# A list scheduler that plans with spare time for transfers and for the engines beside TensorE

## Chip, core and metric

The kernel runs on one core of a Trainium2 chip. The metric is device time in microseconds (us), the median of three runs. TensorE (PE) does the matmuls, VectorE (DVE), ScalarE (ACT) and GpSimd (POOL) do the element-wise work, and SyncE (SP) does no arithmetic here: its queue issues the transfers (DMA), one after the other.

## What is computed

```python
# attention with a feature map, 4 batches x 8 heads x 576 positions x 64
phi = lambda x: [exp(p), exp(-p)], p = x @ w_phi - max|x @ w_phi|
x = (phi(q) @ (phi(k).T @ v)) / (phi(q) @ sum(phi(k)))     # -> 2304 x 512
# mixture of 4 experts, weighted by p = domain_probs / sum
out += p[:, e:e+1] * (relu(x @ w1[e]) @ w2[e])             # 512 -> 1024 -> 512
# gated block
y = ((out @ v1) * (out @ v2)) @ w3 @ w_out                 # -> 2304 x 512
```

## The kernel before

The program is written as a list of operations, each with an engine, an estimated duration and the tiles it reads and writes. `Prog.run` plays that list through a small event model (`simulate`) three times and emits the instructions in the order in which the last pass started them. Every engine then works through its own instructions strictly in that order. So the numbers in the model never run on the chip; they only decide what stands behind what.

In the first pass the model takes ready operations by their place in the text. After that, `deadlines` works out for every operation of DVE, ACT, POOL and SP when it is due, backwards from the PE operations that need it, and the next pass takes ready operations by that due time, PE keeping the order of the pass before. A transfer takes its issue time on SP (400 ns), then lands after `BEFORE` + bytes/`RATE` + `AFTER` ns, where the byte counts are partly fitted numbers and not sizes. A tile is taken when its first writer starts and given back after its last reader, so the order decides also when buffers come free.

The stages: attention in the first 200 us, mixed with the first visits of the experts. A visit is one quarter of an expert (visits 0 to 50 with fold steps among them) for one or two pairs of 768 tokens: PE computes `upa`, `upb`, `upc` (seven products instead of eight, so sums are formed by DVE and ACT: tiles `s1`, `s2`, `s5`, lines L865 and L872), ACT and DVE make `h` from them (L897, L899), PE multiplies by the second weights into `dn` (L911), and DVE adds that to `acc` (L932). Weights come by `raw_a`, `raw_b`, `raw_g` (L431, three buffers for all of them) and are split in two parts by ACT (cast, L421) and POOL (L423, with sums L451) into `w_a`, `w_b`, `w_g`. Fold visits multiply w3 by w_out (`psw`, L1012), because the gated block has no function between them. The last visits (51 to 58) are the gated block.

Three kinds of side work are laid among this. The weights of the gated block arrive as 64-bit numbers; 40 half tiles are brought to 32 bits: a load `near` (L463), one ACT step (L466), five DVE steps (L469, L472, L476, L479, L482) and a write `near_v`, `near_w` or `near_wo` back to memory (L485). They are worked on in buffers named `near0` (24 halves), `near1` and `near2` (8 each). The sums of an expert pair, once complete, are transposed in 32x32 blocks by DVE (L940) and written by four strided transfers each (`turned`, L944, 24 for a pair), then loaded back as `xr` (L948). From `xr` ACT and DVE split the tokens into `x..` tiles (L421, L423, L755).

Of the kernel before, what the change touches and what calls it, by code (L numbers as in the profile page):

```python
# [108 lines left out]
class Op:  # L109
    def __init__(self, n, eng, ns, fn, prio, size, port, mode):  # L110
        self.n, self.eng, self.ns, self.fn, self.prio, self.port, self.size = n, eng, ns, fn, prio, port, size
        self.mode = mode
        self.lag = Prog.TAIL.get(eng, 0.0)
        self.values, self.deps, self.next = [], set(), []


class Prog:
# [10 lines left out]


    SYNC = 45.0  # L130
    TAIL = {"PE": 275.0, "DVE": 185.0, "ACT": 200.0, "POOL": 185.0}
    BEFORE, AFTER, RATE, MARGIN = 850.0, 550.0, 330.0, 400.0
    COLD = 4500.0
# [30 lines left out]
    def simulate(self, key, same=0):  # L164

        for o in self.ops:
            o.count = len(o.deps)
            for v in o.values:
                v.left, v.live = 0, False
        for o in self.ops:  # L170
            for v in o.values:
                v.left += 1
        free, turn = {k: [None] * n for k, n in self.bufs.items()}, dict.fromkeys(self.lines, 0)
        self.heirs, slots = {}, dict.fromkeys(self.bufs, -1)
        engines = list(dict.fromkeys(o.eng for o in self.ops))
        ready, busy, port = {e: [] for e in engines}, dict.fromkeys(engines, 0.0), dict.fromkeys(self.OTHER, 0.0)
        mode = [None]
        events, done, served = [(0.0, 0, o.n, o) for o in self.ops if not o.count], [], [0.0]
        heapq.heapify(events)

        def fits(o):
            need, lines = {}, {}
            for v in o.values:
                if not v.live and v.args[2] is not None:
                    k, n = need.get(v.key, 0), lines.get(v.line, 0)
                    if len(free[v.key]) <= k or v.order != turn[v.line] + n:
                        return False
                    need[v.key], lines[v.line] = k + 1, n + 1
            return True

        def take(o, now):
            for v in o.values:
                if not v.live:
                    v.live = True
                    turn[v.line] += 1
                    v.slot = slots[v.key] = slots[v.key] + 1
                    if v.args[2] is not None:
                        self.heirs[free[v.key].pop(0)] = v
            o.start, o.end = now, now + o.ns
            if o.eng == "PE" and now < self.COLD:  # L200
                o.end += min(o.ns, (self.COLD - now) / 2)
            if o.eng == "PE" and o.mode != mode[0]:
                o.end += self.SWITCH
                mode[0] = o.mode
            busy[o.eng] = o.end
            if o.port:
                port[o.eng] = now + o.port if o.port > 1 else o.end - self.EARLY[o.eng]
            if o.eng == "SP":
                served[0] = max(o.end + self.BEFORE, served[0]) + o.size / self.RATE
                o.lag = served[0] + self.AFTER - o.end  # L210
            done.append(o)
            heapq.heappush(events, (o.end, 2, o.n, o))
            heapq.heappush(events, (o.end + o.lag, 1, o.n, o))

        def choose(e, now):
            held, late, got = [], None, None
            while ready[e] and got is None:
                item = heapq.heappop(ready[e])
                if not fits(item[2]):
                    held.append(item)  # L220
                elif item[2].port and port[self.OTHER[e]] > now:
                    if late is None:
                        late = item
                    else:
                        held.append(item)
                else:
                    got = item
            if got is None and late is not None:
                got, late = late, None
            if late is not None:  # L230
                held.append(late)
            if same and e == "PE" and got is not None and got[2].mode != mode[0]:
                near = [x for x in ready[e] if x[0] <= got[0] + same and x[2].mode == mode[0] and fits(x[2])]
                if near:
                    held.append(got)
                    got = min(near)
                    ready[e].remove(got)
                    heapq.heapify(ready[e])
            for item in held:
                heapq.heappush(ready[e], item)  # L240
            return got and got[2]

        while events:
            now = events[0][0]
            while events and events[0][0] <= now:
                _, kind, _, o = heapq.heappop(events)
                if kind == 0:
                    heapq.heappush(ready[o.eng], (key(o), o.n, o))
                elif kind == 1:
                    for v in o.values:  # L250
                        v.left -= 1
                        if not v.left:
                            free[v.key].append(v)
                    for x in o.next:
                        x.count -= 1
                        if not x.count:
                            heapq.heappush(events, (now + self.SYNC, 0, x.n, x))
            again = True
            while again:
                again = False  # L260
                for e in engines:
                    if busy[e] <= now and ready[e]:
                        o = choose(e, now)
                        if o is not None:
                            take(o, max(now, port[self.OTHER[e]]) if o.port else now)
                            again = True
        assert len(done) == len(self.ops), (len(done), len(self.ops))
        return done
# [15 lines left out]
    def deadlines(self, reuses):  # L284
        due = {}
        for o in sorted(self.ops, key=lambda o: (-o.start, -o.n)):
            t = o.start if o.eng == "PE" else float("inf")
            for x in (*o.next, *reuses[o]):
                if x in due:
                    t = min(t, due[x] - o.ns - o.lag - self.SYNC - (self.MARGIN if o.eng == "SP" else 0.0))  # L290
            due[o] = t
# [47 lines left out]
def fused_kernel(ctx, tc, qT, kT, vt, w_phi, unit, probs, w1, w2, v1, v2, w3T, w_out, out):  # L339
# [5 lines left out]
    V, op = pg.tile, pg.op  # L345
    PE, ACT, DVE, POOL, SP = "PE", "ACT", "DVE", "POOL", "SP"
# [9 lines left out]
    def keep(shape, dt, name, pool="const"):  # L356
        return V(pool, shape, dt, name, 1, name)
# [10 lines left out]
    def mm4(n):  # L368
        return 4 * n / 2.4 + 9

    def dma(fn, nbytes, **kw):
        return op(SP, 400, fn, size=nbytes, **kw)

    wphi = keep([128, FEAT], F32, "wphi", "at")
    wst = keep([128, FEAT], F32R, "wst", "at")
# [5 lines left out]
    turned = [keep([DM, PW], F32, f"turned{i}", "dram") for i in range(3)]  # L381
# [539 lines left out]
    def expert_down(v, i, c, t, hs):  # L921

        for g in range(3):
            ps = down(wb[v], hs, g, f"{v}_{t}{g}")
            share = lambda g=g: pn()[:, (i * 2 + t) * 3 + g, c // NQ:c // NQ + 1]
            if c == first[i]:
                sums[i, t, g] = V(("acc", "acc2")[i % 2], [128, DM], F32, "acc", 6, f"acc{i}_{t}{g}")
            a = sums[i, t, g]
            if c == first[i]:
                op(ACT, act(DM, False) + 90, lambda a=a, ps=ps, share=share: nc.scalar.mul(a(), ps(), share()), reads=[ps, pn], writes=[a], after=start.get("S", ()))  # L930
            else:
                op(DVE, dve(DM) + 61, lambda a=a, ps=ps, share=share: nc.vector.scalar_tensor_tensor(  # L932
                    out=a(), in0=ps(), scalar=share(), in1=a(), op0=ALU.mult, op1=ALU.add
                ), reads=[ps, pn], writes=[a])
            work()
        if c == last[i]:
            x = xraw(i + 3)
            for g in range(3):
                a, o = sums[i, t, g], t * TB + g * 128
                op(DVE, dve(DM), lambda a=a: nc.vector.transpose(out=a(), in_=a()), writes=[a], port=True)  # L940
                work()
                for s in range(4):
                    rows = slice(s * 32, s * 32 + 32)
                    dma(lambda a=a, o=o + s * 32, rows=rows: nc.sync.dma_start(  # L944
                        out=turned[i]().rearrange("(q r) t -> r q t", r=32)[:, :, o:o + 32],
                        in_=a()[rows].rearrange("r (q c) -> r q c", c=32),
                    ), 65536, reads=[a], fills=[turned[i]])
            dma(lambda: nc.sync.dma_start(  # L948
                out=x()[:, :, t * TB:t * TB + TB],
                in_=turned[i]().rearrange("(d p) t -> p d t", p=128)[:, :, t * TB:t * TB + TB],  # L950
            ), 3 << 18, reads=[turned[i]], fills=[x])
            work()
# [264 lines left out]
```

## Time and profile before

| | |
|---|---|
| median of 3 runs | 1231.28 us (1231.13 to 1233.2) |
| profiled execution, own time | 1232.33 us |
| its span, first to last instruction | 1230.5 us |
| mean granted TensorE clock | 0.998 |
| busy: PE, DVE, ACT, POOL | 99%, 71%, 48%, 46% |
| DMA, mean | 103 GB/s |

The span is 1.83 us shorter than that execution's own time; the rest lies around the program. PE is the engine to watch: whatever keeps it from starting its next matmul adds to the time, and nothing else does.

### The profile page before, as it was taken

To read this page: it belongs to the slowest core of one execution; us is meant where nothing else is said; L and a number is where in the kernel's file an instruction comes from. 1 tells how busy PE (TensorE), PEld (TensorE's weight loads), DVE (VectorE), ACT (ScalarE), POOL (GpSimd) and SP (SyncE) were. 2 spreads that over 40 slices of the span, in tenths; PEclk is the share of its full clock that TensorE was granted. 3 is DMA by queue.
4 is the path that set the end of the run, shared out by engine and by line. 5 is a ranking of instruction groups with operands and counts; after the bars stand their busy time and mean duration, and the time that the engine had idled before them with its cause. 6 is when DMAs were issued, how large, how long until landed. Compare 5 with 4: busy or idle time off the path is not lost.

```text
span 1230.5 us, 21131 instructions
## 1 busy us (share of the span) xinstructions
PE 1213.2 (99%) x8318; PEld 1095.5 (89%) x8318; DVE 874.5 (71%) x1417; ACT 591.4 (48%) x1157; POOL 564.1 (46%) x389
## 2 busy tenths in 40 slices
PE   8999999999999999999999999899999999999998
PEld 7998989899999988998887889798998999999998
DVE  6878778887778779444957798688958668624544
ACT  7999886533333333433534454344444455443321
POOL 4344442433333044445543466566665667425320
PEclk9999999999999999999999999999999999999999
DMA  5644312323333232322274435533321522211002
GB/s 153 215 131 136 118 40 85 104 86 111 112 111 112 89 100 95 112 86 86 78 199 144 158 107 105 178 120 112 111 78 61 137 95 69 86 35 52 1 1 103
DMA packets 84947, 126.48 MB, mean 103 GB/s; under 512 B 42864, under 2 KB 51824, under 8 KB 84848
## 3 DMA queue, kind: packets, MB, share of 16 engines
q1 hardware_dynamic: 84704, 125.07, 32.7%
q8 instruction: 65, 1.06, 0.4%
q14 instruction: 34, 0.28, 0.1%
q10 hardware_dynamic: 144, 0.07, 0.0%
HBM read 103.09 MB, written 22.02 MB: 102 GB/s over the span
## 4 chain that ended last, share of the span: by engine, by line
PE 90%; DVE 3%; DMA 3%; SPq 2%; ACT 1%; issue 1%; ACTq 0%; DVEq 0%
PE dn L911 37%; PE upa L842 14%; PE upb L842 6%; PE upc L842 3%; PE num L679 3%; PE psw L1012 3%; PE up L842 3%; PE kvp L584 2%; PE Pq L651 1%; PE upa_3b L842 1%; PE upa_3a L842 1%; PE upa_5b L842 1%; PE upa_4a L842 1%; PE upa_5a L842 1%; PE upa_4b L842 1%; SPq L944 1%
## 5 line engine op out<-in xcount | busy, mean ns | idle before, releaser
L911 PE MATMUL dn<-w_b,h 128*128 128x512 f32 x1728 | 413.9, 392 | 1.2 <-DVE acc L932 1.1
L911 PEld LDWEIGHTS dn<-w_b,h 128*128 128x128 f32 x1728 | 323.0, 188 | 65.0 <-DVE acc L932 2.1
L423 POOL TENSOR_TENSOR w_a<-raw_a,w_a 128x768 fp32r<-128x768 f32 (+2 forms) x86 | 180.2, 2097 | 229.0 <-ACT w_a L421 195.4
L932 DVE SCALAR_TENSOR_TENSOR acc<-dn,pn,acc 128x512 f32<-128x512 f32 x270 | 200.5, 745 | 63.9 <-PE dn L911 61.6
L423 POOL TENSOR_TENSOR w_b<-raw_b,w_b 128x1024 fp32r<-128x1024 f32 x47 | 119.8, 2549 | 226.4 <-ACT w_b L421 194.9
L842 PE MATMUL upa<-x_T,w_a 128*128 128x384 f32 x792 | 160.4, 338 | 7.7 <-ACT s L865 5.3
L842 PEld LDWEIGHTS upa<-x_T,w_a 128*128 128x128 f32 x792 | 139.6, 188 | 13.2 <-ACT s L865 6.8
L421 ACT CAST w_a<-raw_a 128x1024 fp32r<-128x1024 f32 (+2 forms) x95 | 85.1, 897 | 108.4 <-POOL raw_a L451 37.1
L662 POOL PARTITION_ALL_REDUCE M<-Ps x64 | 83.6, 1344 | 103.5 <-ACT Ps L659 97.0
L451 POOL TENSOR_TENSOR raw_a<-raw_a 128x256 f32<-128x256 f32 x140 | 116.1, 829 | 21.6 <-DVE acc L932 6.5
L421 ACT CAST w_b<-raw_b 128x1024 fp32r<-128x1024 f32 x59 | 62.1, 1052 | 100.7 <-PE dn L911 73.9
L911 PE MATMUL dn<-w_b,g 128*128 128x512 f32 x426 | 101.9, 390 | 0.0
L911 PEld LDWEIGHTS dn<-w_b,g 128*128 128x128 f32 x426 | 79.6, 188 | 14.7
L865 ACT COPY s<-upa 128x384 f32<-128x384 f32 x88 | 42.1, 480 | 45.1 <-PE upa L842 44.8
L469 DVE TENSOR_SCALAR near<-near 128x512 int32<-128x512 int32 x40 | 34.0, 851 | 40.9 <-ACT near L466 40.8
L872 DVE TENSOR_TENSOR upc<-upc,s 128x384 f32<-128x384 f32 x44 | 24.7, 561 | 49.0 <-PE upc L842 39.7
L842 PE MATMUL upa<-x_B,w_a 128*128 128x384 f32 x264 | 54.0, 339 | 0.0
L842 PE MATMUL upb<-x_B,w_a 128*128 128x384 f32 x264 | 53.1, 336 | 0.0
L842 PE MATMUL upc<-x_B,w_a 128*128 128x384 f32 x264 | 53.1, 335 | 0.0
L842 PE MATMUL upb<-x_T,w_a 128*128 128x384 f32 x264 | 52.9, 334 | 0.0
L670 ACT ACTIVATE Eq<-Ps 128x256 f32<-128x256 f32 (+3 forms) x128 | 49.5, 441 | 7.2 <-DVE Ps L665 5.5
L992 DVE TENSOR_TENSOR oacc<-dn,oacc 128x512 f32<-128x512 f32 x53 | 36.1, 687 | 21.6 <-PE dn L911 21.5
(222 smaller groups left out, 2140.9 us busy)
## 6 DMA issues: line engine op xcount, KB each, us to landing
raw_a<-w SPq DMA_DIRECT2D x35, 512.0 KB, 3.9
raw_b<-w SPq DMA_DIRECT2D x35, 512.0 KB, 3.6
near<-w3T SPq DMA_DIRECT2D x16, 512.0 KB, 3.7
raw_b<-near_wo SPq DMA_DIRECT2D x16, 512.0 KB, 4.1
near<-v SPq DMA_DIRECT2D x16, 512.0 KB, 4.5
vx<-vt SPq DMA_DIRECT2D x16, 330.0 KB, 3.4
kr<-kT SPq DMA_DIRECT2D x15, 320.0 KB, 3.3
turned<-acc SPq DMA_DIRECT2D x72, 64.0 KB, 2.1
```

What stands on the lines that cost most here:

```text
L421: lambda: op(ACT, act(n, sbuf), lambda: nc.scalar.copy(out=hi(), in_=raw[1]()), reads=[*raw[:1], *raw[2:]], fills=[w], after=after),
L423: lambda: op(eng, ns, lambda: e.tensor_tensor(out=lo(), in0=raw[1](), in1=hi().bitcast(F32), op=ALU.subtract), reads=[raw[0], w, *raw[2:]] ...
L451: ops.append(lambda to=to, a=a, b=b, how=how: op(eng, ns, lambda: e.tensor_tensor(out=raw()[:, to], in0=raw()[:, a], in1=raw()[:, b], op=h ...
L662: op(POOL, 250 + 3.65 * n, lambda M=M, Ps=Ps: nc.gpsimd.partition_all_reduce(M(), Ps(), channels=128, reduce_op=bass_isa.ReduceOp.absmax), ...
L670: op(ACT, act(n), lambda a=a, E=E, Ps=Ps: nc.scalar.activation(out=E()[:, a], in_=Ps(), func=AF.Exp, scale=1.0 - 2 * a), reads=[Ps], fills ...
L679: nc.tensor.matmul(num()[c * 64:c * 64 + 64, 2 * t + h if t < nt else 2 * t], E()[:, a, o:o + 64], KV()[:, a, h], start=a == 0, stop=a == ...
L842: nc.tensor.matmul(ps(), w()[:, a, i, kk * 128:kk * 128 + 128], x()[:, j, kk], start=first and n == 0, stop=last and n == total - 1, skip_ ...
L865: op(ACT, act(TB, False), lambda: nc.scalar.copy(out=t(), in_=ps()), reads=[ps], writes=[t], after=start["C"])
L911: nc.tensor.matmul(ps(), hs[fc]()[:, x, t * 128:(t + 1) * 128], w()[:, fc * 2:fc * 2 + 2, y], start=fc == 0 and n == 0, stop=fc == 1 and n ...
L932: op(DVE, dve(DM) + 61, lambda a=a, ps=ps, share=share: nc.vector.scalar_tensor_tensor(out=a(), in0=ps(), scalar=share(), in1=a(), op0=ALU ...
L992: op(DVE, dve(DM), lambda a=a, ps=ps: nc.vector.tensor_tensor(out=a(), in0=ps(), in1=a(), op=ALU.add), reads=[ps], writes=[a])
L1012: nc.tensor.matmul(ps(), wa[v]()[:, k, a, f * 128:f * 128 + 128], wb[v]()[:, 2 * k:2 * k + 2, b], start=g == 0 and k == 0 and n == 0, stop ...
```

## The change

Three numbers of the model are changed, none of the arithmetic. For operations started after 205 us of the model's time, a transfer's result is taken to be there 1000 ns later, and an operation of DVE, ACT or POOL to last 3% longer. At all times a `turned` write is given 570 ns of issue and 130,000 bytes, where it had 400 ns and 65,536.

```diff
     SYNC = 45.0
+    STEADY, SPARE, SLOW = 205000.0, 1000.0, 1.03
...
             o.start, o.end = now, now + o.ns
+            if now > self.STEADY and o.eng not in ("PE", "SP"):
+                o.end = now + o.ns * self.SLOW
...
                 served[0] = max(o.end + self.BEFORE, served[0]) + o.size / self.RATE
-                o.lag = served[0] + self.AFTER - o.end
+                o.lag = served[0] + self.AFTER - o.end + (self.SPARE if now > self.STEADY else 0.0)
...
-    def dma(fn, nbytes, **kw):
-        return op(SP, 400, fn, size=nbytes, **kw)
+    def dma(fn, nbytes, ns=400, **kw):
+        return op(SP, ns, fn, size=nbytes, **kw)
...
-                    ), 65536, reads=[a], fills=[turned[i]])
+                    ), 130000, ns=570, reads=[a], fills=[turned[i]])
```

Every engine has the same instructions as before. The orders are the same up to about 212 us of the profile, and differ from there on. After the change line numbers from `simulate` on are 1 to 3 higher. In the rows below the last number of a name is a running number of the tile; the digits before it are the visit, the pair and the part.

ACT in visits 39 to 41, before; `near2` is the first half worked on in that buffer.

```order
L897 ACTIVATE h39_2_10_8540<-upa39_2_8396 128x384
L421 CAST w_b40_8568<-raw_b40_8289 128x4x256
L466 ACTIVATE near2_8525<-near2_8525 128x512
L865 COPY s2_40_2_8580<-upa40_2_8492 128x384
L897 ACTIVATE h40_2_00_8592<-upc40_2_8571 128x384
L897 ACTIVATE h40_2_11_8619<-s5_40_2_8527 128x384
```

The same stretch of ACT now:

```order
L868 COPY s2_40_2_8549<-upa40_2_8496 128x384
L900 ACTIVATE h40_2_00_8576<-upc40_2_8542 128x384
L900 ACTIVATE h40_2_11_8583<-s5_40_2_8536 128x384
L424 CAST w_a41_8490<-raw_a41_8368 128x4x256
...
L900 ACTIVATE h41_2_11_8730<-s5_41_2_8668 128x384
L469 ACTIVATE near2_8670<-near2_8670 128x512
L900 ACTIVATE h41_2_01_8779<-upb41_2_8646 128x384
```

The `near2` step has moved behind the drains of visit 40 and most of those of visit 41, 14 places in all.

DVE in visit 32, before, around the third half in `near1`:

```order
L476 TENSOR_SCALAR near1_7335<-near1_7335 128x512
L479 SCALAR_TENSOR_TENSOR near1_7335<-near1_7335 128x512
L899 SCALAR_TENSOR_TENSOR h32_1_01_7610<-upb32_1_7526,h32_1_01_7610 128x384
L899 SCALAR_TENSOR_TENSOR h32_1_10_7614<-upa32_1_7513,h32_1_10_7614 128x384
L482 TENSOR_TENSOR near1_7335<-near1_7335 128x512
L872 TENSOR_TENSOR upc32_2_7627<-upc32_2_7627,s1_32_2_7596 128x384
L872 TENSOR_TENSOR s5_32_2_7623<-upa32_2_7577,s5_32_2_7623 128x384
```

And now (L472 is the first of the five steps, L475 the second):

```order
L902 SCALAR_TENSOR_TENSOR h32_1_10_7618<-upa32_1_7505,h32_1_10_7618 128x384
L875 TENSOR_TENSOR upc32_2_7620<-upc32_2_7620,s1_32_2_7595 128x384
L875 TENSOR_TENSOR s5_32_2_7613<-upa32_2_7571,s5_32_2_7613 128x384
L902 SCALAR_TENSOR_TENSOR h32_2_00_7639<-upc32_2_7620,h32_2_00_7639 128x384
L472 TENSOR_SCALAR near1_7355<-near1_7355 128x512
L875 TENSOR_TENSOR upb32_2_7584<-upb32_2_7584,s2_32_2_7628 128x384
L902 SCALAR_TENSOR_TENSOR h32_2_11_7650<-s5_32_2_7613,h32_2_11_7650 128x384
L475 SCALAR_TENSOR_TENSOR near1_7355<-near1_7355 128x512
```

The sums that PE waits for (`upc32_2`, `s5_32_2`) now stand ahead of the whole third half, where they stood behind its last step.

SP from the sums of pair 1 to the first load into `near2`, before:

```order
L944 DMA turned1_8367<-acc1_00_3918 32x16x32 x4
L431 DMA raw_a41_8384<-w1 128x1024
L944 DMA turned1_8367<-acc1_01_3926 32x16x32 x4
L944 DMA turned1_8367<-acc1_02_3953 32x16x32 x4
...
L431 DMA raw_b41_8473<-w2 128x1024
...
L944 DMA turned1_8367<-acc1_12_3989 32x16x32 x4
L948 DMA xr4_8517<-turned1_8367 128x4x384
L463 DMA near2_8525<-v1 128x1024 x2
L948 DMA xr4_8517<-turned1_8367 128x4x384
L431 DMA raw_a42_8608<-w1 128x1024
```

And now:

```order
L434 DMA raw_a41_8368<-w1 128x1024
L488 DMA near_v21_8238<-near1_7355 128x512
L434 DMA raw_b41_8455<-w2 128x1024
L947 DMA turned1_8524<-acc1_00_3916 32x16x32 x4
L434 DMA raw_a42_8564<-w1 128x1024
...
L434 DMA raw_b42_8628<-w2 128x1024
L947 DMA turned1_8524<-acc1_10_3968 32x16x32 x4
L951 DMA xr4_8659<-turned1_8524 128x4x384
L466 DMA near2_8670<-v1 128x1024 x2
L947 DMA turned1_8524<-acc1_11_3980 32x16x32 x4
```

The weight loads `raw_b41`, `raw_a42` and `raw_b42` stand ahead of most of the strided writes, and the `near2` loads behind `raw_b42`.

## Rows read from the trace of the kernel before

**Rows 1.** Busy time by stage: stretch, its length, busy us (instructions) per engine, granted clock, DMA

```profile
205.00:625.00 420.00, 420.00 (x2098) 379.10 (x2098) 311.97 (x472) 167.66 (x283) 168.16 (x106) 1.00 0.32 101
625.00:700.00 75.00, 70.43 (x333) 59.87 (x332) 49.05 (x72) 30.84 (x53) 34.09 (x22) 1.00 0.56 171
700.00:760.00 60.00, 60.00 (x300) 54.05 (x300) 54.20 (x73) 28.38 (x47) 37.94 (x23) 1.00 0.36 106
760.00:790.00 30.00, 26.29 (x123) 23.28 (x122) 17.18 (x27) 10.39 (x17) 15.67 (x12) 0.94 0.67 188
790.00:950.00 160.00, 158.41 (x796) 143.19 (x795) 127.29 (x174) 70.45 (x115) 103.40 (x72) 1.00 0.29 95
```

**Rows 2.** Waits of PE: who it waited for, us in total, times, longest

```profile
PE upa L842 <- ACT s L865: 5.3, 3, 3.7
PE upa L842 <- DVE s L872: 2.4, 3, 1.0
...
PE dn L911 <- DVE acc L932: 1.1, 2, 0.6
```

**Rows 3.** Timeline of PE, 636 to 649 us: start, us, operation, count, idle before

```profile
644.96 0.50 PE L1012 MATMUL psw<-w_b,w_a 128*128 128x512 f32 x1 [0.83 <-POOL w_b L423]
646.22 2.57 PE L1012 MATMUL psw<-w_b,w_a 128*128 128x512 f32 x10 [0.76 <-POOL w_a L423]
```

**Rows 4.** Timeline of SP, 620 to 634 us

```profile
625.76 0.43 SPq L431 DMA_DIRECT2D raw_a<-w  x1
```

**Rows 5.** Timeline of DVE, 655 to 675 us

```profile
663.23 1.96 DVE L482 TENSOR_TENSOR near<-near 128x512 f32<-128x512 f32 x1
```

**Rows 6.** Chain that ended last, 615 to 700 us: start, us, what

```profile
666.18 1.31 PE upa L842 x6
...
681.44 4.37 DMA near_v<-near
...
686.54 0.38 ACT s L865
...
698.58 1.06 PE upa L842 x6
```

**Rows 7.** Timeline of all engines, 755 to 782 us

```profile
758.18 2.92 PE L911 MATMUL dn<-w_b,h 128*128 128x512 f32 x12
...
774.16 0.66 ACT L466 ACTIVATE near<-near 128x512 f32<-128x512 f32 x1 [4.71 <-DMA near<-v]
...
775.25 1.95 PE L842 MATMUL upa<-x_T,w_a 128*128 128x384 f32 x6 [3.71 <-ACT s L865]
...
777.00 3.91 PE L911 MATMUL dn<-w_b,h 128*128 128x512 f32 x12
```

**Rows 8.** Chain that ended last, 755 to 785 us

```profile
767.65 6.49 DMA near<-v
...
780.90 1.04 PE upa L842 x6
```

**Rows 9.** Chain that ended last, 830 to 850 us

```profile
839.87 2.61 DVE near L469
```

**Rows 10.** Chain that ended last, 925 to 940 us

```profile
930.29 1.22 DVE x_B L423
```

**Rows 11.** DMA issues: count, KB each, median us from issue to landing

```profile
raw_a<-w SPq DMA_DIRECT2D x35, 512.0 KB, 3.9
...
near<-v SPq DMA_DIRECT2D x16, 512.0 KB, 4.5
...
near_v<-near SPq DMA_DIRECT2D x16, 256.0 KB, 3.3
```

**Rows 12.** One line's instructions: duration ns min/median/max, first and last start us

```profile
L944 SPq DMA_DIRECT2D turned<-acc x72: 302/504/2394, 609.4 to 980.7; - x72
L482 DVE TENSOR_TENSOR near<-near x40: 675/692/2786, 229.5 to 887.0; 128x512 f32<-128x512 f32 x40
```

**Rows 13.** Busy time of ACT on line 466 alone, by stage: stretch, length, busy us (instructions), clock, DMA

```profile
205.00:625.00 420.00, 15.99 (x24) 1.00 0.32 101
```

## The prediction

> **What bounds the kernel now.** I read four views: busy time by stage, the waits of PE, the chain that ended last, and the timeline at each of PE's waits.
>
> The stages show where there is anything to gain [rows 1]. From 205 to 625 us PE is busy 420.00 of 420.00 us, and again 60.00 of 60.00 from 700 to 760. It idles 75.00 - 70.43 = 4.57 us from 625 to 700, 30.00 - 26.29 = 3.71 from 760 to 790 and 160.00 - 158.41 = 1.59 from 790 to 950: 9.87 us in all. The first 205 us have their own gaps, but the order there is the same as before. So the change can win only in 625 to 950 us, and it can lose wherever PE is now full.
>
> Nine waits make up these 9.87 us. The waits of PE name three on ACT's `s` (5.3 us, one of them 3.7), three on DVE's `s` (2.4) and one or two on `acc` [rows 2]; two more are on POOL's split of a fold's weights, 0.83 and 0.76 us [rows 3]. The engine that is named is never the cause. The chain and the timelines show what held it:
>
> - At 775 us ACT had `s2_40_2` to do, but stood 4.71 us in front of a `near` step whose load was not there [rows 7]. That load took 6.49 us [rows 8]. PE lost 3.71 us.
> - At 686 us the same with a write: ACT's `near` step reuses a buffer that a `near_v` write was still reading, 4.37 us, and the next item, `s`, came 0.38 us before PE went on [rows 6].
> - At 666 us DVE did the last `near` step for 1.96 us ahead of the sums that PE needed [rows 5]; at 843 us a first `near` step took 2.61 us [rows 9]; at 934 us a split of `x_B` took 1.22 us ahead of `upc` [rows 10].
> - At 645 us POOL was late because `raw_a32` had been issued at 625.76 us, behind four writes of `turned0_11` [rows 4].
>
> So these are not missing resources. They are places where work with time to spare stands, in an engine's fixed order, just ahead of work without any. Why the model put it there can be read too. It lets a `near` load land 3.7 us after issue (850 + 770000/330 + 550 ns), a `raw_a` load after 2.9 and a `near_v` write after 2.2; the medians are 4.5, 3.9 and 3.3 [rows 11]. It gives a `turned` write 400 ns of SP, and the median is 504 [rows 12].
>
> **The change, part by part.** The spare 1000 ns makes the three landings 4.7, 3.9 and 3.2 us, which is what the medians are. The `turned` write at 570 ns of issue is now a little over its median. Both are corrections of the model towards the trace. The 3% on DVE, ACT and POOL are 20 ns on a `near` step of 0.6 us: small, but they favour urgent work a little more.
>
> What the new order does at the nine waits, in the order of the program:
>
> 1. 645 us: `raw_a32` stands ahead of the `turned0_11` writes and saves up to four of them, 4 x 0.504 = 2.0 us or more. The split of `w_b31`, behind it on ACT and POOL, comes earlier by about as much, and the two waits were 0.83 + 0.76 = 1.6. They go, with little to spare.
> 2. 657 to 673 us, three waits on DVE: the `near1` steps now stand behind the sums of visit 32 (shown above for the third half). All three go.
> 3. 686 us: ACT's step for that half moved seven places, behind `s2_35_1`. It goes.
> 4. 775 us: ACT's step moved 14 places, behind all drains of visit 40. It goes, with the clock that fell after it.
> 5. 843 us: that first step stands 19 places later on DVE, behind `s5_44_2`. It goes.
> 6. 934 us: `upc50_2` and its ACT step are now ahead of the `x4_B00` split. It goes.
>
> What these waits cost in all is more than the idle time. Six matmuls of `upa` take 1.04 to 1.06 us in a running stream [rows 6, 8] and 1.31 just after a wait [rows 6], so each restart costs about 0.26; eight of the nine make 2.1. After the ninth the granted clock fell to its lower level (0.94 as a mean of 760 to 790 us [rows 1]): the next six took 1.95 for 1.04 [rows 7, 8], and twelve of `dn` 3.91 for 2.92 [rows 7], 0.9 + 1.0 = 1.9 us more. Sum: 9.87 + 2.1 + 1.9 = 13.9 us. That is all there is to win.
>
> What is added: nothing in work, but everything that moved is now late somewhere. On SP the `near` loads and writes and the `turned` writes stand behind weight loads that wait for one of three buffers, so SP holds them until the buffer is free. The first `near2` load was issued at 767.65 us and now waits for `raw_b42`, a visit later; the chain of eight halves behind it ends about a visit later too. That costs nothing as long as the last `near_v` write, which still stands ahead of all loads that read it (`raw_a53`, `raw_g53`, `raw_a54`, `raw_g54`), and the reload `xr5`, still ahead of `raw_b54`, come before visit 53. Their cover is the stretch from 900 us on, with no `near` work left in it; without it each us of delay would be a us of PE. On ACT and DVE the moved steps stand in front of the next visit's drains instead of this one's. There I see four thin places: the two `psw` of visit 31, where the split ends within some 2 us of its use; the third and the fourth half in `near1`, whose ACT steps follow the previous half's write by little more than its 3.3 to 4.4 us [rows 6, 11]; and the first half in `near2`, whose load, at 4.5 to 6.5 us [rows 8, 11], lands about when ACT comes to it. The trace of before cannot show whether they hold. A place that holds costs nothing, one that does not cost 0.8 us, as the waits on POOL did [rows 3], and at the far end 3.7 us [rows 7]. I take 0.8 for each, the nearest in kind, 3.2 in all.
>
> One row speaks against such moves: DVE's `near` step of 0.69 us has once taken 2.79 [rows 12], and which ones stretch depends on what POOL does beside them, which the move changes. The Trainium skill, SBUF — State Buffer, Who interferes with whom, says that a DVE instruction with two SBUF inputs contends with a GpSimd instruction that reads SBUF, and that the second to issue blocks until the first is done; by that rule moved steps meet other POOL splits and new stalls of up to 2.1 us (2.79 - 0.69) stand wherever they land; with one ahead of a drain in every second of 16 halves that is 8 x 2.36 = 18.9 us back, the slower case below. The trace agrees that steps stretch, but the 24 halves of `near0` fall in 205 to 625 us [rows 13], where PE lost nothing, so a stretch by itself is covered. I leave the sum as it is.
>
> Sum against the profiled execution: its own time 1232.33 (span 1230.5 and 1.83 around it) - 13.9 + 3.2 = 1221.6. The median of the runs is 1.05 lower than that execution: 1220.6, rounded to **1220.5 us**.
>
> **Rivals.**
>
> *The waits come back at other places, half of them.* All of 625 to 950 us is packed: DVE is busy 54.20 of 60 us from 700 to 760 and 127.29 of 160 from 790 to 950 [rows 1], and without its waits PE runs through these visits faster, which leaves the side work less time. The thin places would cost 3.2, and four more as much as the ones at 666 and 686 (some 1 us each with the restart): 1231.3 - 13.9 + 3.2 + 4 = 1224.6, about 1225.
>
> *The change doesn't do what it says.* The added spare is the same for all transfers, and the weight loads get earlier due times with the `near` ones. The order could then be only different, not safer, with as many waits as before: about 1231. Against it stands that each of the nine waits is dissolved in the new order by a move of the very operation that caused it.
>
> *Slower: stretched `near` steps ahead of drains.* If at most of the 16 halves in `near1` and `near2` a stretched step stands directly ahead of a sum that PE needs, each costs 2.1 us and a restart, 2.36. It outweighs the 13.9 us, and the 2.5 that a measurement needs, from the seventh on (7 x 2.36 = 16.5); at nine of 16 the time is 1231.3 - 13.9 + 21.2 = 1238.6. In the order I see urgent sums ahead of `near` steps, not behind them, and before only two of the nine waits were of that size.
>
> **How the numbers follow.** Forecast 0.62, half back 0.22, as many waits as before 0.09, slower 0.07. The forecast's own range goes from 1217 (no thin place bites, 1231.3 - 13.9 = 1217.4) to 1224 (four bite at double). The range of 8 in 10 takes in most of the second case: 1217 to 1228. A measurement of this kernel tells about 0.2%, 2.5 us, from no change; faster than that is below 1228.8, which holds the first two cases: 0.84. Same 0.09, slower 0.07.
>
> **What would show it.** Right: PE busy over 74 of the 75 us from 625 us on, no wait of 3 us on `s` and no fall of the granted clock near 775 us, the places at 843 and 934 us without idle time, and remaining waits of under 1 us at `psw`, at the `near1` steps or at the first `near2` step. The first 205 us and the stretch after 1050 us read as before. Wrong: ACT in front of a `near` step for longer than 2 us with PE waiting behind; new waits from 205 to 625 us, where the order changed without need; a weight load that PE waits for because SP stood at a `near` write; or a second fall of the clock.

## The result, and the profile after

The changed kernel takes 1217.88 us (median of 4 runs, 1217.61 to 1218.1), the kernel before in the same session 1231.2 (1230.61 to 1233.2): a ratio of 0.9889, interval 0.9872 to 0.9906. Faster by 1.1%, as forecast (1220.5), and near the low end of the range. The profiled execution took 1217.66 us, with a span of 1215.9 (before: 1232.33 and 1230.5).

Busy time by stage, after; the columns are those of [rows 1]:

```profile
205.00:625.00 420.00, 420.00 (x2097) 378.99 (x2097) 316.00 (x471) 167.01 (x283) 167.50 (x106) 1.00 0.31 101
625.00:700.00 75.00, 75.00 (x372) 67.04 (x371) 53.23 (x75) 33.60 (x56) 36.29 (x22) 1.00 0.57 177
700.00:760.00 60.00, 60.00 (x296) 53.51 (x295) 54.03 (x73) 28.84 (x47) 36.30 (x24) 1.00 0.29 96
760.00:790.00 30.00, 30.00 (x152) 27.05 (x151) 21.63 (x34) 12.55 (x20) 18.57 (x14) 1.00 0.82 204
790.00:950.00 160.00, 160.00 (x812) 145.91 (x811) 123.99 (x180) 71.06 (x116) 105.86 (x74) 1.00 0.31 102
```

PE is busy for the whole of 745 us; 4.57, 3.71 and 1.59 us of idle time are gone, and the granted clock is at its upper level throughout (0.94 before from 760 to 790 us). The first rows of PE's waits, after, all lie before 205 us:

```profile
PE kvp L509 <- ACT KV L615: 1.1, 1, 1.1
PE kvp L509 <- DVE warm L516: 1.0, 1, 1.0
PE dn L914 <- DVE acc L935: 0.5, 1, 0.5
```

Where in the program the time was won shows from the `upa` matmuls, first of before, then of after: count, ns (min/median/max), first and last start.

```profile
L842 PE MATMUL upa<-x_T,w_a x792: 331/335/522, 205.2 to 939.2; 128*128 128x384 f32 x198
```

```profile
L845 PE MATMUL upa<-x_T,w_a x792: 331/335/339, 205.2 to 924.6; 128*128 128x384 f32 x198
```

The first starts at the same time, the last 14.6 us earlier, and that is the whole difference of the spans (1230.5 - 1215.9). From the last one to the end both take 291.3 us. The medians differ by less, 13.3 us, since the profiled execution of before was 1.1 us above its median.

The places of the nine waits. At 645 us the twelve `psw` now run as one stream (timeline of PE, after):

```profile
643.68 2.91 PE L1015 MATMUL psw<-w_b,w_a 128*128 128x512 f32 x12
```

The load of the weights whose split they waited for is now issued at 623.95 us, where it was 625.76 [rows 4] (timeline of SP, after):

```profile
623.95 0.43 SPq L434 DMA_DIRECT2D raw_a<-w  x1
```

The step of ACT that held PE at 686 us belonged to the fifth half in `near1`, counting the `near` steps of ACT from 636 us on. The fifth now starts without idle time, behind drains of `h` (timeline of ACT, after):

```profile
688.09 0.66 ACT L469 ACTIVATE near<-near 128x512 f32<-128x512 f32 x1
```

That wait is gone. A new one of the same kind stands at the fourth half, which before started at 670.53 us without idle time: ACT stands 4.10 us in front of it, for a write (same view):

```profile
671.38 0.66 ACT L469 ACTIVATE near<-near 128x512 f32<-128x512 f32 x1 [4.10 <-DMA near_v<-near]
671.95 1.03 ACT L424 CAST w_a<-raw_a 128x1024 fp32r<-128x1024 f32 x1
673.56 1.06 ACT L424 CAST w_b<-raw_b 128x1024 fp32r<-128x1024 f32 x1 [0.58 <-PE psw L1015]
674.52 0.62 ACT L424 CAST w_a<-raw_a 128x512 fp32r<-128x512 f32 x1
678.71 0.48 ACT L868 COPY s<-upa 128x384 f32<-128x384 f32 x1 [3.57 <-PE upa L845]
```

What is queued behind it is casts of weights for later; the next drain, `s`, starts 7.3 us after the `near` step and has to wait for PE, not PE for it. At this half the order has not avoided a wait, but what the wait delays is harmless. The first half in `near2` comes at a quiet place as well. The loads of its first two halves were issued from 774.52 us on and took nearly as long as the late one of before (6.49 us [rows 8]; issue to landing, SP's `near` loads from 774 to 776 us, after):

```profile
DMA to landing us min/median/max: 6.1/6.2/6.4
```

But ACT comes to the step only when the first of them has landed. It starts without idle time, and behind it ACT waits 3.84 us for PE:

```profile
781.39 0.66 ACT L469 ACTIVATE near<-near 128x512 f32<-128x512 f32 x1
785.90 0.50 ACT L900 ACTIVATE h<-upb 128x384 fp32r<-128x384 f32 x1 [3.84 <-PE dn L914]
```

### The profile page after: what moved, and what is told of

Same layout as the page of the kernel before. It is cut to its first block, busy times and chain, and to the rows that moved or that the text cites. A ratio compares the mean times of both kernels' runs of the same rounds, so it can differ in the third digit from the quotient of the medians.

```text
span 1215.9 us, 21121 instructions
## 1 busy us (share of the span) xinstructions
PE 1209.8 (99%) x8318; PEld 1095.9 (90%) x8318; DVE 876.6 (72%) x1417; ACT 590.2 (49%) x1157; POOL 561.3 (46%) x389
## 4 chain that ended last, share of the span: by engine, by line
PE 99%; DMA 1%; ACT 0%; DVE 0%; issue 0%
PE dn L914 41%; PE upa L845 15%; PE upb L845 8%; PE upc L845 4%; PE psw L1015 4%; PE num L682 3%; PE up L845 3%; PE kvp L587 2%; PE Pq L654 2%; PE upa_3a L845 1%; PE upa_3b L845 1%; PE upa_5b L845 1%; PE upa_5a L845 1%; PE upa_4a L845 1%; PE upa_4b L845 1%; PE P L574 1%
## 5 line engine op out<-in xcount | busy, mean ns | idle before, releaser
L875 DVE TENSOR_TENSOR upc<-upc,s 128x384 f32<-128x384 f32 x44 | 24.8, 563 | 61.8 <-PE upc L845 42.7
L900 ACT ACTIVATE h<-upb 128x384 fp32r<-128x384 f32 x44 | 21.6, 490 | 65.9 <-PE dn L914 59.9
```

## The experiments

Three theories were put against each other. **Landing**: the plan let transfers land too early, the `near` ones above all, and correcting that removed the waits (the prediction's reason). **Margin**: any slack in the plan, on whatever work, keeps side work out of PE's gaps. **Lottery**: every new order draws its own waits, and before was a poor draw. The first three expectations name a fourth, **writes**: the strided writes, planned too cheap on SP, pushed loads late. Each kernel below has the arithmetic of the kernel before; only the order differs, and in the last one also the number of matmuls that fill time. All were timed against it (its median was 1231.2 to 1232.3).

| run | spare, ns | longer | turned | us | ratio, interval |
|---|---|---|---|---|---|
| spare_alone | 1000 | - | as before | 1218.26 | 0.9888, 0.9871 to 0.9904 |
| slow_alone | - | 3% | as before | 1220.79 | 0.9909, 0.9894 to 0.9924 |
| turned_alone | - | - | 570 ns, 130,000 B | 1220.2 | 0.9906, 0.9891 to 0.992 |
| near_spare | 1000 on `near` only | - | as before | 1224.27 | 0.9944, 0.9926 to 0.9961 |
| rest_spare | 1000 on all but `near` | - | as before | 1221.02 | 0.9907, 0.9891 to 0.9924 |
| spare_10ns | 10 | - | as before | 1230.24 | 0.998, 0.9969 to 0.9991 |
| spare_100ns | 100 | - | as before | 1221.17 | 0.9908, 0.9893 to 0.9923 |
| slow_0p1 | - | 0.1% | as before | 1223.59 | 0.9926, 0.9903 to 0.995 |
| spare_minus_1000 | -1000 | - | as before | 1234.01 | 1.0012, 1.0 to 1.0024 |
| slow_minus_3 | - | -3% | as before | 1228.63 | 0.9973, 0.9961 to 0.9984 |
| full_3000 | 3000 | 3% | as changed | 1218.56 | 0.9889, 0.9874 to 0.9904 |
| full_from_0 | 1000, from 0 us | 3%, from 0 us | as changed | 1224.2 | 0.9936, 0.9921 to 0.995 |

**Each part alone.** Edits, against the change, of the three kernels in turn:

```diff
-    STEADY, SPARE, SLOW = 205000.0, 1000.0, 1.03
+    STEADY, SPARE, SLOW = 205000.0, 1000.0, 1.0
-                    ), 130000, ns=570, reads=[a], fills=[turned[i]])
+                    ), 65536, reads=[a], fills=[turned[i]])
```

> Of the change only the 1000 ns on landings is kept. Landing theory (the waits came from a plan in which transfers land 0.9 to 1.1 us too early): most of the gain stays, 1218 to 1222 us, no wait near 775 us. Writes theory (the strided writes, planned too cheap on SP, pushed loads late): little stays, 1227 to 1231. Lottery theory (any disturbance of the plan deals a new set of waits, of which the change drew a good one): anywhere from 1217 to 1235, with waits at new places.

```diff
-    STEADY, SPARE, SLOW = 205000.0, 1000.0, 1.03
+    STEADY, SPARE, SLOW = 205000.0, 0.0, 1.03
-                    ), 130000, ns=570, reads=[a], fills=[turned[i]])
+                    ), 65536, reads=[a], fills=[turned[i]])
```

> Only the 3% on DVE, ACT and POOL is kept. Landing theory: the landings are as wrong as before, so most waits stay, 1226 to 1231 us. Writes theory: 1228 to 1231. Lottery theory: anywhere from 1217 to 1235.

```diff
-    STEADY, SPARE, SLOW = 205000.0, 1000.0, 1.03
+    STEADY, SPARE, SLOW = 205000.0, 0.0, 1.0
```

> Only the dearer strided writes are kept. Landing theory: the waits at 645 and, in part, 775 us go, since SP stands at the writes there; those at 657 to 686, 843 and 934 us stay: 1223 to 1229 us. Writes theory: most of the gain, 1218 to 1222. Lottery theory: anywhere from 1217 to 1235.

They gave 1218.26, 1220.79 and 1220.2 us. Against the 1231.72 of before beside them the gains are 13.5, 10.9 and 11.5 us, where the whole change brings 13.3, so they do not add: any one of the three brings over 80% of it, also the 3% and the strided writes, which change no estimate of the side work's own loads. By the expectations the landing theory holds for the first alone: it wanted 1226 or more from the second and 1223 or more from the third. The writes theory holds for the third alone: the other two leave the writes as they were and win as much. The lottery's range takes in all three. ACT's idle time ahead of its `near` step, by what ended it (us, times), first before, then `turned_alone`, then after:

```profile
  DMA near_v<-near: 14.2, 8
  DMA near_w<-near: 9.7, 6
  DMA near<-v: 8.5, 2
```

```profile
  DMA near_v<-near: 14.6, 7
  DMA near_w<-near: 10.2, 6
  DMA near<-v: 3.4, 2
```

```profile
  DMA near_v<-near: 8.0, 3
  DMA near_w<-near: 1.6, 2
  DMA near<-v: 1.3, 1
```

With the `turned` numbers alone ACT stands as long in front of the writes as before (24.8 us for 23.9), and yet PE lost only 0.25 + 1.12 + 0.23 = 1.6 us from 625 to 950 (stages, `turned_alone`):

```profile
625.00:700.00 75.00, 74.75 (x366) 66.10 (x365) 55.09 (x76) 33.90 (x56) 37.78 (x22) 1.00 0.55 176
700.00:760.00 60.00, 58.88 (x290) 52.27 (x289) 50.09 (x72) 27.87 (x45) 37.33 (x25) 1.00 0.38 106
790.00:950.00 160.00, 159.77 (x806) 144.69 (x806) 125.51 (x175) 69.47 (x114) 106.56 (x74) 1.00 0.30 96
```

Late transfers alone do not set PE's waits.

**The spare split by transfer.** First on the `near` loads and writes alone, then on every other transfer. The edits are against the kernel before; the line of `o.lag` is the same in both, and line numbers there are 5 higher than before:

```diff
-                o.lag = served[0] + self.AFTER - o.end
+                o.lag = served[0] + self.AFTER - o.end + (o.spare if now > self.STEADY else 0.0)
...
+    def dma(fn, nbytes, ns=400, spare=0.0, **kw):
+        o = op(SP, ns, fn, size=nbytes, **kw)
+        o.spare = spare
+        return o
...
-            ), 770000, writes=[raw], after=start["C"]),
+            ), 770000, spare=1000.0, writes=[raw], after=start["C"]),
...
-            lambda: dma(lambda: nc.sync.dma_start(out=near[key, i]()[:, half], in_=f()), 1 << 18,
+            lambda: dma(lambda: nc.sync.dma_start(out=near[key, i]()[:, half], in_=f()), 1 << 18, spare=1000.0,
```

> The 1000 ns is given to the loads and writes of the near halves alone, and nothing else of the change is kept. Landing theory, in the form of the prediction (near steps stood ahead of drains because their own transfers were planned too short): nearly all of the gain, 1218 to 1222 us. If it is the spare of the weight loads that counts, 1226 to 1231. Lottery theory: anywhere from 1217 to 1235.

```diff
+    def dma(fn, nbytes, ns=400, spare=1000.0, **kw):
...
+            ), 770000, spare=0.0, writes=[raw], after=start["C"]),
...
+            lambda: dma(lambda: nc.sync.dma_start(out=near[key, i]()[:, half], in_=f()), 1 << 18, spare=0.0,
```

> The spare of 1000 ns on all transfers but the near loads and near writes: the complement of near_spare; no 3%, turned as before. Landing theory (the near steps came too early because their transfers were planned too early): this part helps only at the raw_a splits, two waits of the nine: 1229 to 1231. Margin theory (any slack in the plan, on whatever work, keeps side work out of PE's gaps): about as good as near_spare, 1220 to 1226. Lottery (every new order draws its own waits, before was an average draw): anywhere from 1221 to 1235.

The `near` transfers, which stood behind the waits at 686 and 775 us, bring it to 1224.27; all the others, with the `near` landings planned as early as ever, to 1221.02. By the landing theory the first should have come to 1222 or less and the second have been left at 1229 or more; it missed both. Margin and lottery take in the second. In `near_spare` two waits of PE are left, and they show both ways in which ACT is held (first its timeline, then PE's):

```profile
649.17 0.66 ACT L471 ACTIVATE near<-near 128x512 f32<-128x512 f32 x1 [4.22 <-DMA near_v<-near]
...
799.11 1.04 ACT L426 CAST w_a<-raw_a 128x1024 fp32r<-128x1024 f32 x1 [3.06 <-POOL raw_a L456]
800.06 0.47 ACT L870 COPY s<-upb 128x384 f32<-128x384 f32 x1
```

```profile
652.75 1.32 PE L847 MATMUL upa<-x_T,w_a 128*128 128x384 f32 x6 [2.18 <-ACT s L870]
...
800.59 1.31 PE L847 MATMUL upb<-x_B,w_a 128*128 128x384 f32 x6 [2.49 <-ACT s L870]
```

The 4.22 us at 649 are nearly the 4.10 of the changed kernel at 671; here `s` follows soon and PE pays 2.18, there it follows 7.3 us later and PE pays nothing. At 799 us it is a cast of weights that stands ahead of the drain, held by POOL's sum of a weight tile.

What made ACT's step at 649 us late was only in part the landing of its write (chain that ended last, `near_spare`):

```profile
638.50 2.00 DVE near L481
640.52 2.78 DVE near L484
643.32 1.69 DVE near L487
645.03 4.07 DMA near_v<-near
```

The three DVE steps, the last of the five, whose medians in this run are 0.42, 0.69 and 0.69 us, took 4.7 us longer than that, with POOL at weight splits from 637.76 to 644.46 us, and only then was the write issued. The spare on landings does not tell the plan of that.

**Nudges.** Numbers too small to correct anything, each by itself, `turned` as before; the line is shown against the change:

```diff
+    STEADY, SPARE, SLOW = 205000.0, 10.0, 1.0
```

> Landings 10 ns later and nothing else of the change: no correction worth the name, but the order differs in 99 places on ACT and 235 on DVE. Landing theory: as before, 1229 to 1233 us. Lottery theory (the order before was an unlucky draw, and nearly any other is better): 1217 to 1226 us.

```diff
+    STEADY, SPARE, SLOW = 205000.0, 100.0, 1.0
```

> The spare alone, at 100 ns: between spare_10ns (1230.2) and spare_alone (1218.3). Landing theory: the landings are still 0.7 us too early at the medians, nothing is corrected: 1229 to 1232. Margin theory, graded by the dose: 1226 to 1231. Lottery: any value from 1221 to 1235; a value under 1222 would say that the size of the spare counts for nothing.

```diff
+    STEADY, SPARE, SLOW = 205000.0, 0.0, 1.001
```

> The side engines 0.1% slower in the plan and nothing else, again no correction, 192 places on ACT and 392 on DVE. Landing theory: 1229 to 1233 us. Lottery theory: 1217 to 1226 us, and not the same waits as with 10 ns.

They gave 1230.24, 1221.17 and 1223.59 us: three orders, 9 us apart, from inputs that say almost the same as before. The 100 ns leave the three landings 0.3 to 0.6 us short of their medians (counted as in the next section) and still win 11 us; by its expectation a value under 1222 says that the size of the spare counts for nothing. The 0.1% lie in the lottery's range too. The 10 ns do not: 1230.24 is where the landing theory had it and above the lottery's 1217 to 1226, so not nearly every other order is much better than before. With 10 ns the wait at 775 us is there still, built as before [rows 7, 8] (chain that ended last, `spare_10ns`; its profiled execution, of 1226.85 us, is the fastest of its ten):

```profile
766.69 6.37 DMA near<-v
...
773.08 0.66 ACT near L469
...
774.67 0.39 ACT s L868
```

Part of the scatter goes with the granted clock. The four executions of `slow_0p1` took 1221.12 and 1221.62 us at a mean clock of 1.000 and 0.999, and 1225.56 and 1226.54 at 0.998 and 0.997, so its median lies between two groups. The changed kernel and the other orders that reach 1221.02 or less show 1.000 in every execution.

**The other sign.** The same numbers taken away, `turned` as before:

```diff
+    STEADY, SPARE, SLOW = 205000.0, -1000.0, 1.0
```

> The correction with the wrong sign: landings 1000 ns earlier in the plan, so a near load after 2.7 us where the median is 4.5. Landing theory: more and longer waits than before, 1236 us or more. Pure lottery theory: 1217 to 1231 us like any other draw. Both at work: above the two tiny changes, say 1224 to 1236.

```diff
+    STEADY, SPARE, SLOW = 205000.0, 0.0, 0.97
```

> The side engines 3% faster in the plan, the wrong sign. Landing theory: about as before or a little slower, 1230 to 1235 us. Pure lottery theory: 1217 to 1231 us.

With 1000 ns less than before the time is 1234.01, with engines 3% shorter 1228.63. The first is the slowest of all, though barely slower than before, and its longest waits are new ones on `acc` (waits of PE from 205 us on, `spare_minus_1000`):

```profile
PE dn L914 <- DVE acc L935: 5.6, 4, 2.7
```

It fits only the expectation that had both at work (1224 to 1236): landing alone wanted 1236 or more, lottery alone 1231 or less. The second is 3.6 us faster than the before beside it, clear of noise, though the plan has less slack: that is the lottery's range and not the landing theory's.

A pure lottery has no reason to put all eight orders with a real addition (1000 or 3000 ns, 3%, the `turned` numbers; two of them below) at 1217.9 to 1224.3. The four slowest of the 14 orders are before, 10 ns and the two reduced ones; if all 14 were equal draws, none of the eight would be among the four slowest in about 1.5 of 100 cases (an estimate, since several of the eight share an addition). A pure margin has no reason for 1221.17 at 100 ns, or for a gain with 3% taken away. That both are at work is the likelier reading; how much each gives is not shown.

**More of it.** A spare three times as large in the whole change:

```diff
-    STEADY, SPARE, SLOW = 205000.0, 1000.0, 1.03
+    STEADY, SPARE, SLOW = 205000.0, 3000.0, 1.03
```

> The whole change with a spare of 3000 ns for 1000. Landing theory: the plan is now wrong the other way, loads are issued earlier than needed and hold buffers longer, so one or two new waits: 1219 to 1223. Margin theory: PE without a wait from 205 to 950 us, the floor again: 1217 to 1219.5. Lottery: a new draw, 1221 to 1235.

1218.56 us: the floor again, from another order, as margin expected and under the ranges of the other two. Between 205 and 950 us PE idles only 0.99 us, all of it before 625. From 790 to 950 (stages, `full_3000`):

```profile
790.00:950.00 160.00, 160.00 (x812) 145.92 (x811) 135.40 (x180) 69.69 (x114) 106.93 (x74) 1.00 0.33 107
```

DVE is busy 135.40 us there, more than the 127.29 of before [rows 1], and PE waits for none of it.

**From the start.** An attempt to go below the changed kernel, where after 205 us nothing is left to win:

```diff
-    STEADY, SPARE, SLOW = 205000.0, 1000.0, 1.03
+    STEADY, SPARE, SLOW = 0.0, 1000.0, 1.03
```

> The whole change from the start of the program instead of from 205 us. After 205 us nothing is left to win, so a gain can only come from the gaps of PE in the first 205 us. Margin theory: those are waits for the first loads, which no order makes land sooner, but a few late ones may go: 1213 to 1219. Lottery: the first 205 us get a new draw, 1212 to 1226. Landing theory: as with margin after 205 us, and before it the 1000 ns put loads in a worse order when the queue is the limit: 1218 to 1226.

1224.2 us: worse than the change, above what margin expected and within the other two's ranges. The first 205 us pay for it (matmuls of two lines, `full_from_0`):

```profile
L509 PE MATMUL kvp<-fill_z x107: 249/253/381, 1.0 to 108.3; 128*128 128x208 bf16 x107
L845 PE MATMUL upa<-x_T,w_a x792: 331/335/443, 210.8 to 931.0; 128*128 128x384 f32 x198
```

The changed kernel runs 52 of these `kvp<-fill_z` matmuls, whose product is of a tile of zeros and which only fill time; here there are 107. The first `upa` comes 5.6 us late (210.8 for 205.2). A filler's 0.253 us overlap the next one's: ten in a row take 1.05 us (timeline of PE, `full_from_0`):

```profile
33.50 1.05 PE L509 MATMUL kvp<-fill_z 128*128 128x208 bf16 x10
```

Counted in the two traces from each start to the next one on PE, with the idle time behind it, the fillers take 12.8 us up to that `upa`, and 7.0 in the changed kernel; all other matmuls ahead of it take 197.1 and 197.2. So the 5.6 us are filler, and not the other order of the real work. The program emits fillers where its plan sees PE idle, so a plan that is too cautious there buys filler that takes time which real work could use.

No kernel beat the changed one; `spare_alone` and `full_3000` are equal to it within what can be measured.

## Why the prediction was right, and where it was not

**The nine waits.** Right in all six points: none is left, nor is the fall of the clock. Where the move can be followed, it is the one that was named: `raw_a` is issued 1.8 us earlier, the fifth `near1` half and the first `near2` half stand behind drains, and the `near2` load took 6.1 us where the late one of before took 6.49. The sum said that 13.9 us were to be won (9.87 idle, 2.1 restarts, 1.9 clock); the spans differ by 14.6. The trace of before shows where they lie, counted from each start of a matmul to the next and against the means of after. The nine waits cost 12.3 us, 2.45 more than their idle time. The lower clock cost 1.6. Four hesitations of 0.07 to 0.23 us, near 638, 652, 663 and 737 us, cost 0.6; they are too short to be listed as waits. 0.1 is left. So the two added terms were off by some 0.3 us each, in opposite senses, and the hesitations were missed. The 0.26 us per restart came out near the measured 2.45 / 9 = 0.27 by luck: in the chain that ended last the 1.04 us of a running six [rows 6, 8] begin at the end of the matmuls before, the 1.31 after a wait at the six's own start, and counted from its own start a running six lasts 1.20 us.

**The four thin places, 3.2 us.** Mis-sized: they cost nothing, and this is why the time came out 2.6 us under the forecast. The two `psw` of visit 31 run without a gap (643.68 us above); ACT did stand 4.10 us at the fourth `near1` half, as feared, but with casts behind it and 3.57 us of waiting for PE at the next drain; the third started without idle time, and the first `near2` half found its load there, landed some 0.8 us before. Pricing a place by what a wait on POOL cost elsewhere missed that a late step costs PE only what is left after the idle time of its engine at the next drain. What stands behind a step can be read from the new order, which was at hand, and the prediction did not use it for the price.

**Why the model put the work there.** This step is the one that failed in part: "Both are corrections of the model towards the trace. The 3% on DVE, ACT and POOL are 20 ns on a `near` step of 0.6 us: small". The sizes are not like for like. The model's 3.7, 2.9 and 2.2 us (`near`, `raw_a`, `near_v`) begin when SP's 400 ns of issue end, and the trace's medians at the start of the issue. Counted alike, with no transfer ahead, the plan of before had 4.1, 3.3 and 2.6 us against 4.5, 3.9 and 3.3: 0.4 to 0.7 us too early, and not 0.8 to 1.1. The spare takes them to 5.1, 4.3 and 3.6, past the medians. The landings as traced after are 3.7, 3.8 and 3.0 us for `raw_a`, `near` and `near_v` (medians), which the spare covers:

```profile
raw_a<-w SPq DMA_DIRECT2D x35, 512.0 KB, 3.7
...
near<-v SPq DMA_DIRECT2D x16, 512.0 KB, 3.8
...
near_v<-near SPq DMA_DIRECT2D x16, 256.0 KB, 3.0
```

But the 3% alone won 10.9 us, the `turned` numbers alone 11.5, the spare without the `near` transfers 11.1, and 100 ns, no correction at all, 11.0. The correction is sufficient and not needed; what it shares with the others is that the order is drawn anew, in most of them with slack in it.

**The rival "only different, not safer"**, at 0.09. As a forecast it failed: the time was not 1231. As a mechanism it was underrated. The three nudges have a mean of 1225.0 us, about half of the way from 1232 to 1218, so by these three about half of the gain would have come from leaving an unlucky order, and the rest from the margin. Three draws from 1221 to 1230 make that split rough, and it stays open. The reason given against it, that each wait was dissolved by a move of the operation that caused it, is true of the one order that was at hand and says nothing of the next.

**The rival "half back"** found its case in `near_spare` (1224.27, two waits of 2.2 and 2.5 us) and `slow_0p1` (1223.59), not in the change.

**The rival "stretched steps".** Did not come in the changed kernel. DVE's last `near` step still reaches 2.78 us, once right ahead of two sums (timelines of DVE, POOL and PE, after):

```profile
838.86 2.85 POOL L426 TENSOR_TENSOR w_b<-raw_b,w_b 128x1024 fp32r<-128x1024 f32 x1
...
839.48 2.78 DVE L485 TENSOR_TENSOR near<-near 128x512 f32<-128x512 f32 x1
...
842.18 0.55 DVE L875 TENSOR_TENSOR upc<-upc,s 128x384 f32<-128x384 f32 x1
...
842.25 1.20 PE L845 MATMUL upa<-x_T,w_a 128*128 128x384 f32 x6
...
843.28 2.92 PE L914 MATMUL dn<-w_b,h 128*128 128x512 f32 x12
```

DVE's step ends 0.55 us after POOL's split. The Trainium skill, SBUF — State Buffer, Who interferes with whom, says that the second of two such instructions blocks until the first is done; this row agrees. PE at that point had six `upa` and twelve `dn` of its own order to do that needed neither sum, so the stretch cost nothing. The prediction was right to leave it out of the sum. In `near_spare` such stretches did cost, by another way than the rival's: they made a write late, ACT stood for it, and PE lost 2.18 us.

## What to carry to other kernels

When in-order engines are filled from a planned order, look at each long wait for what stands behind it, not for how long it is: a 4.1 us wait ahead of casts was free, one of 4.2 ahead of a drain cost 2.2. In these runs slack on any of the plan's estimates helped. Give such a plan some, then try a few more values, because a plan with none can be an unlucky draw, and a change of 10 or 100 ns in one number moves the time by 2 to 11 us here. Judge a scheduler's change against several such nudges, and not by one before and one after.

## What the runs showed that was not expected

Slack that costs nothing: the `near` work comes later (its last DVE step starts at 897.7 us for 887.0 [rows 12]), and no use of it waits. The DVE steps also stretch less often in the new order: from 625 to 950 us 12 `near` steps of DVE last over 1.5 us where 20 did (counted from the trace), with the same longest, as these rows show beside [rows 12]:

```profile
L947 SPq DMA_DIRECT2D turned<-acc x72: 302/504/2367, 611.1 to 973.4; - x72
L485 DVE TENSOR_TENSOR near<-near x40: 674/683/2782, 228.3 to 897.7; 128x512 f32<-128x512 f32 x40
```

The strided write's issue still has a median of 504 ns, so the 570 of the plan changed no transfer, only what stands around it. And it is an engine that works strictly in order through which a late transfer reaches PE: the Trainium skill, PSUM — Partial Sum Buffer, Engine vs sequencer instructions, calls the queues of ScalarE, VectorE and GpSimd strict FIFO. The rows at 649 us in `near_spare` agree: ACT stood 4.22 us for a write that only a `near` step needed, while PE waited 2.18 us for the `s` behind it.
